# Half-batch loads, pairwise crossbar transposes and a reordered MLP queue in a linear-attention and gated-MLP kernel

## The chip, the cores and the metric

The kernel runs on one core of a Trainium2 chip. A core has a matrix engine (TensorE, PE in the profile, with its weight loads as PEld), a vector engine (VectorE, DVE), an engine for activations (ScalarE, ACT), a general one (GpSimd, POOL) and SyncE (SP), which here only issues DMAs. Each engine runs its own instructions in order and waits on semaphores for the others. The metric is the device time of one execution in microseconds: 302.88 us, the median of three runs (301.88 to 304.17). The profiled execution took 299.19 us and its span, from the first instruction to the last, is 297.4 us.

## What is computed

Attention with a feature map, over 8 batches, 8 heads, 576 tokens and head size 64, and then an MLP whose gate mixes the tokens:

```python
def phi(x):                                    # x: (8, 8, 576, 64), w_phi: (64, 128)
    proj = np.einsum('bhsd,df->bhsf', x, w_phi)
    proj = proj - np.max(np.abs(proj), axis=-1, keepdims=True)
    return np.concatenate([np.exp(proj), np.exp(-proj)], axis=-1)
q_p, k_p = phi(q), phi(k)
kv  = np.einsum('bhsf,bhsd->bhfd', k_p, v)
z   = np.sum(k_p, axis=2)
num = np.einsum('bhsf,bhfd->bhsd', q_p, kv)
den = np.einsum('bhsf,bhf->bhs', q_p, z)[..., None] + 1e-06
x   = (num / den)                              # then heads side by side: (8, 576, 512)

h = np.maximum(x @ w_in, 0.0)                  # w_in: (512, 1024)
u, v = h[..., :512], h[..., 512:]
v_n = (v - mean(v)) / np.sqrt(var(v) + 1e-06)  # over the last axis
v_s = np.einsum('ts,bsd->btd', w_spatial, v_n) + b_spatial[None, :, None]
out = (u * v_s) @ w_out                        # w_out: (512, 512)
```

All inputs and the output are float32 in memory; the kernel computes its matmuls in bfloat16.

## The kernel before

The tokens of a batch are split in a main part of 512 and a tail of 64. Two batches (a group) share one tail tile. The attention is a list of 36 units: a unit is a pair of heads of one batch's main part (four units a batch) or the tail of a group. A software pipeline walks over them in steps, and each step does one stage of several units: the keys and queries of unit i, the sums (kv) of unit i-2, the attention of unit i-3, the output transpose of unit i-4.

```python
units = []
for g in range(G):                       # G = 4 groups of two batches
    if g > 0:
        units.append(dict(pair=False, g=g, i=len(units)))       # tail
    for b in (2 * g, 2 * g + 1):
        for pj in range(NP):             # NP = 4 pairs of heads
            units.append(dict(pair=True, g=g, b=b, pj=pj, i=len(units)))
# ...
ORDER = (("keys", 0.375), ("queries", 0.25), ("attention", 0), ("sums", 0.25),
         ("next", 0.125), ("features", 0), ("out", 0), ("maxima", 0))
LAGS = dict(next=-1, maxima=1, features=2, sums=2, attention=3, out=4)
```

q and k are loaded by GpSimd's DMA queue, which also turns them into bfloat16, one DMA for each operand and batch. v goes through SyncE's queue. From batch 2 on (XB = 2), q and k are transposed by the DMA crossbar, with one transpose for each operand and batch. Batches 0 and 1 and the tails are transposed on TensorE. `pin` is a helper that keeps an instruction in program order, which is why many lines of the profile carry its line, L61.

```python
def pin(start):                                                    # L61
    return lambda *a, **kw: tc.keep_in_program_order(start(*a, **kw))

def alloc(b):
    st[b] = dict(
        q=ld.tile([P, H, NB * D], BF16, tag="q_bf", name="q_bf", bufs=2),
        k=ld.tile([P, H, NB * D], BF16, tag="k_bf", name="k_bf", bufs=2),
        v=ld.tile([P, H * NB, D], FP32, tag="v_f", name="v_f"),
    )

def load(x, b, h0=0, n=H):
    if b not in st:
        alloc(b)
    pin(nc.gpsimd.dma_start)(out=st[b][x][:, h0:h0 + n], in_=main_ap(q if x == "q" else k, b, h0, n))

def cross(b):
    d = st[b]
    for x in ("k", "q"):
        d[x + "T"] = ld.tile([P, 2 * H, P], BF16, tag=x + "T_b", name=x + "T_b", bufs=2)
        pin(nc.sync.dma_start_transpose)(out=d[x + "T"], in_=d[x].rearrange("p h x -> p (h x)"))

def q_even(u):                      # a copy of half of qT, through SyncE's queue
    u["qE"] = qts[u["i"] % len(qts)]
    pin(nc.sync.dma_start)(out=u["qE"][0:D], in_=st[u["b"]]["qT"][0:D, 4 * u["pj"]:4 * u["pj"] + 4, :])
```

The keys and queries are projected on TensorE (`ps`, L247). VectorE takes the maxima of their absolute values (L259, L273), ScalarE the exponentials (`kf` L262, `qf` L346, `em` L282), and GpSimd multiplies v by the key's scale `em` (`vs` L287, the tail's `vst` L302) and prepares the queries' maxima (`mhl` L276, L277). Then come the sums `pv` (L359, L361) and the attention `pn` (L379), the normalization of x on VectorE (L369, L370), and the transpose of x, which for most units is also a crossbar transpose on SyncE's queue:

```python
def a_x_t(u):
    # ...
    dst = st[u["b"]]["xT"][:, u["pj"], :]
    if XX <= u["i"] < NU - 4:                                      # XX = 9, NU = 36
        nc.sync.dma_start_transpose(out=dst.rearrange("p (n t) -> p n t", n=NB),   # L388
                                    in_=u["x"].rearrange("p n h d -> p (n h d)"))
        return
    # ... else four transposes on TensorE and a copy by VectorE (L393, L394)
```

When the last pair of a batch has its x, the batch's MLP goes into a queue of tasks. They are woven between the attention's stages, with the number of tasks for each stage set by their cost. The tasks are v (`pv` L428, relu `vr` L430 on ScalarE, statistics L431 on VectorE), the root and the normalization on GpSimd (`rs` L439, `vn` L445), u (`pu` L482, relu L484 on ScalarE), the spatial matmuls (`ps` L503, L504, times u on VectorE, L506) and the output (`po` L528, copied by L531, stored by L537).

```python
def b_ln(b):
    d = st[b]
    rstd = root(d["mv"], slice(0, P), NB)
    for j in range(NB):
        normalize(d["vn"][:, j, :], d["vr"][j], rstd[:, j, :])     # GpSimd, L445

def b_tasks(b):
    # outs: output tasks of batch b-1; vs, us, ss: four each of v, u, spatial
    ts = outs[:1] + [(MM, lambda: b_v_tail(g, [bl]))] + vs[:2] + outs[1:2] + vs[2:]
    ts.append((0.0, lambda: b_ln(b)))
    ts += outs[2:3] + us[:1] + outs[3:] + us[1:2]
    if b == 0:
        ts += [(0.3, lambda i=i: transpose_spatial(i)) for i in range(NB + 1)]
    ts += us[2:3] + ss[:1] + us[3:] + ss[1:2] + [(MM / 2, lambda: b_u_tail(g, [bl]))] + ss[2:]
    ts.append((MS / 2, lambda: b_s_tail(g, [bl])))
    return ts + (out_tasks(b) if b == B - 1 else [])
```

Loads and crossbar transposes are placed at the ends of steps, counted from the first unit of their batch:

```python
AT, AB, XP = 5, 6, 3
at(1, load, "k", 1)
at(1, load, "q", 1)
at(1, load_v, 1, nc.sync)
# ... weights at steps 2 to 4
for u in units:
    if not u["pair"] and u["g"] > 0:
        at(u["i"] - AT, load_tail, "k", u["g"])
        at(u["i"] - AT + 1, load_tail, "q", u["g"])
        at(u["i"] - AT + 1, load_tail, "v", u["g"])
    if u["pair"] and u["pj"] == 0 and u["b"] > 1:
        at(u["i"] - AB, load, "k", u["b"])
        at(u["i"] - AB + 1, load, "q", u["b"])
        at(u["i"] - AB + 1, load_v, u["b"], nc.sync)
        if u["b"] >= XB:
            at(u["i"] - XP, cross, u["b"])
for u in units:
    if merged(u):
        at(u["i"] - 1, q_even, u)
for i in range(NU + 4):
    step(i)
    for f in io.get(i, []):
        f()
```

Of the kernel before, what the change touches and what calls it, by code (L numbers as in the profile page):

```python
# [8 lines left out]
FP32 = mybir.dt.float32  # L9
BF16 = mybir.dt.bfloat16  # L10
# [6 lines left out]
def kernel(  # L17
# [15 lines left out]
    nc = tc.nc  # L33

    B, H, S, D = q.shape
# [4 lines left out]
    P = 128  # L40
    KC = DM // P
    NP = H // 2
    NB = 4
    T0 = NB * P
    TL = S - T0
# [14 lines left out]
    def pin(start):  # L60
        return lambda *a, **kw: tc.keep_in_program_order(start(*a, **kw))  # L61
# [9 lines left out]
    st = {}  # L71
    gs = {}

    XB = 2

    def alloc(b):
        st[b] = dict(
            q=ld.tile([P, H, NB * D], BF16, tag="q_bf", name="q_bf", bufs=2),
            k=ld.tile([P, H, NB * D], BF16, tag="k_bf", name="k_bf", bufs=2),
            v=ld.tile([P, H * NB, D], FP32, tag="v_f", name="v_f"),  # L80
        )

# [4 lines left out]
            v=ld.tile([P, H, D], FP32, tag="v_tl", name="v_tl", bufs=1),  # L87
        )

    def load(x, b, h0=0, n=H):  # L90
        if b not in st:
            alloc(b)
        pin(nc.gpsimd.dma_start)(out=st[b][x][:, h0:h0 + n], in_=main_ap(q if x == "q" else k, b, h0, n))

    def load_v(b, eng):
        pin(eng.dma_start)(out=st[b]["v"].rearrange("p (h c) d -> p h (c d)", h=H), in_=main_ap(v, b))

    def load_tail(x, g):
        if g not in gs:
# [45 lines left out]
    pin(nc.vector.tensor_scalar)(out=sel, in0=sel1.unsqueeze(2).to_broadcast([P, H, F]), scalar1=-1.0,  # L145
                                 scalar2=None, op0=ALU.mult)
    for x in ("k", "q"):
        pin(nc.vector.tensor_copy)(out=st[0][x][:, 0:2], in_=first[x])
    vst, vnt = [], []
    for i in range(2):  # L150
        t = cpool.tile([P, 2, 2, H, DA], BF16, name=f"vst{i}")
# [10 lines left out]
    load_v(0, nc.sync)  # L162
    for x in ("k", "q", "v"):
        load_tail(x, 0)
    load("k", 0, 2, 2)
    load("q", 0, 2, 2)
    load("k", 0, 4, 4)
    load("q", 0, 4, 4)
# [5 lines left out]
    wspt = ld.tile([TL, S], BF16, tag="kT_b", name="wspt", bufs=2)  # L174
    bsp_row = ld.tile([P, S], FP32, tag="qT_b", name="bsp_row", bufs=2)
# [46 lines left out]

    def q_even(u):
        u["qE"] = qts[u["i"] % len(qts)]
        pin(nc.sync.dma_start)(out=u["qE"][0:D], in_=st[u["b"]]["qT"][0:D, 4 * u["pj"]:4 * u["pj"] + 4, :])

    def a_transpose(u):
        src = st[u["b"]] if u["pair"] else gs[u["g"]]
        if "kT" in src:
            for x in ("kT", "qT"):  # L230
                u[x] = src[x][:, 4 * u["pj"]:4 * u["pj"] + 4, :] if u["pair"] else src[x]
            return
        for x, copy in (("k", nc.vector.tensor_copy if u["i"] < EK else nc.scalar.copy), ("q", nc.vector.tensor_copy)):
            pt = psum.tile([P, 4, P], BF16, tag="bank", name="pt")
            for j in range(4):
                if u["pair"]:
                    blk = src[x][:, 2 * u["pj"] + j // 2, (j % 2) * P:(j % 2 + 1) * P]
# [196 lines left out]
    def root(mv, r, n):  # L434

        var = small.tile([P, NB, 1], FP32, tag="var", name="var")
        rs = small.tile([P, NB, 2], FP32, tag="rs", name="rs")
        nc.gpsimd.tensor_scalar(out=var[r, 0:n], in0=mv[r, 0:n, 1:2], scalar1=1e-6, scalar2=None, op0=ALU.add)
        nc.gpsimd.tensor_tensor(out=rs[r, 0:n, 0:1], in0=var[r, 0:n], in1=neghalf[r, 0:n].unsqueeze(2), op=ALU.pow)  # L439
        nc.gpsimd.tensor_tensor(out=var[r, 0:n], in0=mv[r, 0:n, 0:1], in1=rs[r, 0:n, 0:1], op=ALU.mult)  # L440
        nc.gpsimd.tensor_scalar(out=rs[r, 0:n, 1:2], in0=var[r, 0:n], scalar1=-1.0, scalar2=None, op0=ALU.mult)
        return rs

    def normalize(dst, src, rs):
        nc.gpsimd.tensor_scalar(out=dst, in0=src, scalar1=rs[:, 0:1], scalar2=rs[:, 1:2],  # L445
                                op0=ALU.mult, op1=ALU.add)
# [216 lines left out]
    at(4, load_weight, w_in_bf[:, :, 0:HALF], cols[:, :, 0:HALF])  # L663
    at(4, load_weight, w_out_bf, moe_w_out.rearrange("(kc p) f -> p kc f", p=P))
    for u in units:
        if not u["pair"] and u["g"] > 0:
# [49 lines left out]
```

## Time and profile before

| | |
|---|---|
| median of three runs | 302.88 us (301.88 to 304.17) |
| span of the profiled execution | 297.4 us |
| mean granted TensorE clock | 0.977 |
| GpSimd DMA loads of a whole batch of k or q | 7 + 7, 512 KB each, 8.6 and 8.8 us to landing (median) |
| crossbar transposes of k and q | 6 + 6, 7.1 and 5.6 us to landing (median) |
| crossbar transposes of x | 20, 4.2 us to landing (median) |

"Busy" is the time in which an engine executes; matmuls are pipelined, so a busy PE need not be PE at its peak. The row of the granted clock gives tenths of full speed in 40 slices of the span. A line of a group or a timeline reads: source line, engine, operation, destination <- source, and in brackets the idle time of the engine before it and what ended it. A line of the waits reads: who waited <- for what, the total in us, how many times, and the longest. POOL's or SPq's DMA lines are the issue of a DMA, not the transfer, which is listed as the time to landing.

### The profile page before, as it was taken

The numbers are of one execution on the slowest core, as the hardware profiler recorded it, in microseconds if no ns is written. First come the engines' busy times: TensorE is split into PE (matmuls) and PEld (weight loads), VectorE is DVE, ScalarE is ACT, GpSimd is POOL, SyncE is SP. The second block draws the span as 40 slices with busy tenths as digits, with TensorE's granted clock in tenths as the row PEclk, the third lists the DMA queues.
The fourth block names the chain that finished last, engine by engine and source line by source line (L and its number), as shares of the span: only waits on it lengthen the run. The fifth ranks groups of instructions, "written<-read, shape, count | busy, mean of one in ns | idle before, by whom it ended". The sixth has DMA issues, their size and how long they took to land.

```text
span 297.4 us, 8021 instructions
## 1 busy us (share of the span) xinstructions
PE 259.4 (87%) x3002; PEld 172.6 (58%) x3042; DVE 229.0 (77%) x575; ACT 222.4 (75%) x504; POOL 188.9 (64%) x344
## 2 busy tenths in 40 slices
PE   3277899985999999299999989998999999999893
PEld 2156786761776666066676657565666666554351
DVE  6299998882899989268988978996899987656341
ACT  7669998994499988259888977897789976733421
POOL 8589994399639994736657895589347843421700
PEclk9999999996999999779999999999999999999999
DMA  7979999994824999995906997999422300120205
GB/s 185 234 122 178 210 240 187 137 230 64 127 47 102 227 162 164 175 276 116 210 19 187 219 203 157 250 169 176 101 71 65 99 20 35 73 73 36 106 3 177
DMA packets 83628, 41.90 MB, mean 141 GB/s; under 512 B 50626, under 2 KB 78978, under 8 KB 83588
## 3 DMA queue, kind: packets, MB, share of 16 engines
q1 hardware_dynamic: 56100, 29.90, 45.6%
q0 software_dynamic: 27328, 11.41, 32.4%
q8 instruction: 24, 0.39, 0.6%
q14 instruction: 16, 0.13, 0.1%
q10 hardware_dynamic: 160, 0.07, 0.1%
HBM read 32.85 MB, written 9.44 MB: 142 GB/s over the span
## 4 chain that ended last, share of the span: by engine, by line
PE 52%; POOL 15%; ACT 13%; DVE 8%; DMA 5%; issue 4%; SPq 0%; POOLq 0%; ACTq 0%; DVEq 0%
PE ps L503 9%; PE pv L428 7%; PE po L528 6%; PE pu L482 5%; PE ps L247 5%; ACT kf L262 5%; ACT qf L346 4%; PE pv L359 4%; POOL vn L445 4%; DMA q_tl<-in_q_dram 3%; POOL vst L302 3%; PE pn L379 3%; PE pq L325 2%; PE ps L504 2%; ACT vr L430 2%
## 5 line engine op out<-in xcount | busy, mean ns | idle before, releaser
L287 POOL TENSOR_TENSOR vs<-v_f,em 128x512 bf16<-128x512 f32 x64 | 65.5, 1045 | 28.3 <-ACT em L282 26.9
L262 ACT ACTIVATE kf<-ps 128x512 bf16<-128x512 f32 x144 | 75.8, 637 | 8.1 <-DVE mk L259 7.9
L346 ACT ACTIVATE qf<-pq 128x512 bf16<-128x512 f32 x128 | 66.5, 617 | 7.8 <-PE pq L325 7.3
L259 DVE TENSOR_REDUCE mk<-ps 128x4 f32<-128x512 f32 x72 | 47.8, 678 | 0.9 <-issue 0.2
L273 DVE TENSOR_REDUCE mq<-ps 128x4 f32<-128x512 f32 x62 | 39.8, 680 | 2.0 <-PE ps L247 2.0
L503 PE MATMUL ps<-w_spT,vn 128*128 128x512 bf16 x117 | 34.8, 388 | 7.2 <-POOL vn L445 6.1
L506 DVE TENSOR_TENSOR uT<-ps,uT 128x512 bf16<-128x512 f32 x32 | 22.0, 688 | 22.0 <-PE ps L504 21.8
L428 PE MATMUL pv<-w_in_bf,xT 128*128 128x512 bf16 x116 | 31.3, 384 | 7.0 <-DMA xT<-x 6.1
L430 ACT ACTIVATE vr<-pv 128x512 bf16<-128x512 f32 (+1 forms) x40 | 23.7, 622 | 14.8 <-PE pv L428 12.8
L431 DVE BATCH_NORM_STATS2 stats<-vr 128x6 f32<-128x512 bf16 (+1 forms) x40 | 26.6, 683 | 8.4 <-ACT vr L430 8.0
L482 PE MATMUL pu<-xT,w_in_bf 128*128 128x512 bf16 x120 | 32.3, 382 | 0.5 <-issue 0.2
L528 PE MATMUL po<-w_out_bf,uT 128*128 128x512 bf16 x119 | 31.9, 379 | 0.5
L484 ACT ACTIVATE uT<-pu 128x512 bf16<-128x512 f32 x32 | 19.6, 629 | 15.0 <-PE pu L482 12.9
L359 PE MATMUL pv<-vs,kf 128*128 128x66 bf16 x512 | 24.9, 195 | 0.9 <-ACT kf L262 0.9
L370 DVE TENSOR_TENSOR x<-pn,rc 128x256 bf16<-128x256 f32 x64 | 25.2, 418 | 0.5
L379 PEld LDWEIGHTS <-qf 128*128 128x128 bf16 x512 | 20.7, 98 | 8.2 <-issue 1.4
L445 POOL TENSOR_SCALAR vn<-vr,rs 128x512 bf16<-128x512 bf16 x32 | 24.3, 770 | 0.8
L359 PEld LDWEIGHTS <-kf 128*128 128x128 bf16 x512 | 22.1, 98 | 2.9 <-issue 2.4
L503 PEld LDWEIGHTS <-vn 128*128 128x128 bf16 x128 | 11.7, 98 | 20.3 <-POOL vn L445 11.5
L379 PE MATMUL pn<-kv,qf 128*128 128x66 bf16 x512 | 22.2, 195 | 1.0 <-ACT qf L346 1.0
L428 PEld LDWEIGHTS <-xT 128*128 128x128 bf16 x128 | 12.0, 99 | 18.6 <-DMA xT<-x 6.6
L361 PE MATMUL pv<-vst,kf 128*128 128x66 bf16 x128 | 21.5, 193 | 1.2 <-POOL vst L304 1.2
(128 smaller groups left out, 559.6 us busy)
## 6 DMA issues: line engine op xcount, KB each, us to landing
v_f<-in_v_dram SPq DMA_DIRECT2D x8, 1024.0 KB, 9.9
out_dram<-ob SPq DMA_DIRECT2D x32, 256.0 KB, 2.5
k_bf<-in_k_dram POOLq DMA_DIRECT2D x7, 512.0 KB, 8.6
q_bf<-in_q_dram POOLq DMA_DIRECT2D x7, 512.0 KB, 8.8
qt<-qT_b SPq DMA_DIRECT2D x24, 64.0 KB, 2.8
v_tl<-in_v_dram SPq DMA_DIRECT2D x8, 128.0 KB, 5.9
w_in_bf<-in_moe_w_in_dram POOLq DMA_DIRECT2D x2, 512.0 KB, 8.8
out_dram<-ob SPq DMA_DIRECT2D x8, 128.0 KB, 2.3
```

Of the source, the lines that this page charges most:

```text
L259: nc.vector.tensor_reduce(out=u["mk"][:, hs], in_=pk, axis=AX.X, op=ALU.max, apply_absolute_value=True)
L262: nc.scalar.activation(out=u["kf"][:, s, hs, :], in_=pk, func=AF.Exp, bias=0.0, scale=sc)
L273: nc.vector.tensor_reduce(out=mq[:, 4 * half:4 * half + 4], in_=pq, axis=AX.X, op=ALU.max, apply_absolute_value=True)
L287: nc.gpsimd.tensor_tensor(out=vs[:, s, :, 0:D], in0=st[u["b"]]["v"][:, pj * H:(pj + 1) * H, :], in1=em[:, s, :].unsqueeze(2).to_broadcast( ...
L346: nc.scalar.activation(out=qf[:, s], in_=pq, func=AF.Exp, bias=0.0, scale=sc)
L359: nc.tensor.matmul(out=pv[:, hh, s, :], lhsT=u["kf"][:, s, 4 * hh + c, :], rhs=u["vs"][:, s, 4 * hh + c, :], start=(c == 0), stop=False)
L379: nc.tensor.matmul(out=pn[:, pos, :], lhsT=u["qf"][hh][:, s, pos, :], rhs=d["kv"][:, 2 * u["pj"] + hh, s, :], start=(s == 0), stop=(s == 1))
L428: nc.tensor.matmul(out=pv[r], lhsT=lhs(kc), rhs=w_in_bf[:, kc, HALF:DFF], start=(kc == 0), stop=(kc == KC - 1))
L445: nc.gpsimd.tensor_scalar(out=dst, in0=src, scalar1=rs[:, 0:1], scalar2=rs[:, 1:2], op0=ALU.mult, op1=ALU.add)
L482: nc.tensor.matmul(out=pu, lhsT=w_in_bf[:, kc, dc * P:(dc + 1) * P], rhs=d["xT"][:, kc, :], start=(kc == 0), stop=(kc == KC - 1))
L503: nc.tensor.matmul(out=ps, lhsT=d["vn"][:, sp, cs], rhs=w_spT[:, sp, 0:T0], start=(sp == 0), stop=False)
L528: nc.tensor.matmul(out=po[r], lhsT=lhs(dc), rhs=w_out_bf[:, dc, :], start=(dc == 0), stop=(dc == KC - 1))
```

## The change

It replaces the two rotating whole-batch buffers of q and of k by four half-batch buffers each, taken in turns by name, and loads them by halves, spread over steps. Each pair of heads now has its own crossbar transpose, three steps ahead of its unit, in place of one for the whole batch. v is loaded by halves from batch 2 on. The tails of groups 2 and 3 are loaded one step earlier. In the MLP's queue the normalization is split in four tasks, one ahead of each u task, and all u tasks stand ahead of the spatial ones. The purpose is to free buffers earlier and to shorten what other transfers and GpSimd's other work stand behind.

```diff
     def alloc(b):
         st[b] = dict(
-            q=ld.tile([P, H, NB * D], BF16, tag="q_bf", name="q_bf", bufs=2),
-            k=ld.tile([P, H, NB * D], BF16, tag="k_bf", name="k_bf", bufs=2),
+            q=[None, None], k=[None, None],
 ...
+    def half_tile(x, b, y):
 ...
+        if st[b][x][y] is None:
+            n = f"{x}_bf{(2 * b + y) % 4}"
+            st[b][x][y] = ld.tile([P, 4, NB * D], BF16, tag=n, name=n, bufs=1)
+        return st[b][x][y]
+
+    def load(x, b, y, h0=0, n=4):
+        t = half_tile(x, b, y)
+        pin(nc.gpsimd.dma_start)(out=t[:, h0:h0 + n], in_=main_ap(q if x == "q" else k, b, 4 * y + h0, n))
 ...
-    def cross(b):
-        d = st[b]
-        for x in ("k", "q"):
-            d[x + "T"] = ld.tile([P, 2 * H, P], BF16, tag=x + "T_b", name=x + "T_b", bufs=2)
-            pin(nc.sync.dma_start_transpose)(out=d[x + "T"], in_=d[x].rearrange("p h x -> p (h x)"))
+    def cross(x, u):
+        n = f"{x}T_b{u['b'] % 2}{u['pj']}"
+        u[x + "T"] = ld.tile([P, 4, P], BF16, tag=n, name=n, bufs=1)
+        src = st[u["b"]][x][u["pj"] // 2][:, 2 * (u["pj"] % 2):2 * (u["pj"] % 2) + 2, :]
+        pin(nc.sync.dma_start_transpose)(out=u[x + "T"], in_=src.rearrange("p h x -> p (h x)"))
 ...
-    def b_ln(b):
+    def b_root(b):
+        st[b]["rs"] = root(st[b]["mv"], slice(0, P), NB)
+
+    def b_ln(b, j):
         d = st[b]
-        rstd = root(d["mv"], slice(0, P), NB)
-        for j in range(NB):
-            normalize(d["vn"][:, j, :], d["vr"][j], rstd[:, j, :])
+        normalize(d["vn"][:, j, :], d["vr"][j], d["rs"][:, j, :])
 ...
+        ns = [(0.0, lambda j=j: b_ln(b, j)) for j in range(NB)]
         ts = outs[:1] + [(MM, lambda: b_v_tail(g, [bl]))] + vs[:2] + outs[1:2] + vs[2:]
-        ts.append((0.0, lambda: b_ln(b)))
-        ts += outs[2:3] + us[:1] + outs[3:] + us[1:2]
+        ts.append((0.0, lambda: b_root(b)))
         if b == 0:
             ts += [(0.3, lambda i=i: transpose_spatial(i)) for i in range(NB + 1)]
-        ts += us[2:3] + ss[:1] + us[3:] + ss[1:2] + [(MM / 2, lambda: b_u_tail(g, [bl]))] + ss[2:]
+        for y in range(NB):
+            ts += ns[y:y + 1] + outs[2 + y:3 + y] + us[y:y + 1]
+        ts += [(MM / 2, lambda: b_u_tail(g, [bl]))] + ss
 ...
-    at(1, load, "k", 1)
-    at(1, load, "q", 1)
-    at(1, load_v, 1, nc.sync)
+    at(1, load, "k", 1, 0)
+    at(1, load, "q", 1, 0)
+    at(1, load, "k", 1, 1)
+    at(1, load, "q", 1, 1)
+    at(1, load_v, 1)
 ...
         if not u["pair"] and u["g"] > 0:
-            at(u["i"] - AT, load_tail, "k", u["g"])
-            at(u["i"] - AT + 1, load_tail, "q", u["g"])
-            at(u["i"] - AT + 1, load_tail, "v", u["g"])
-        if u["pair"] and u["pj"] == 0 and u["b"] > 1:
-            at(u["i"] - AB, load, "k", u["b"])
-            at(u["i"] - AB + 1, load, "q", u["b"])
-            at(u["i"] - AB + 1, load_v, u["b"], nc.sync)
-            if u["b"] >= XB:
-                at(u["i"] - XP, cross, u["b"])
+            early = 1 if u["g"] > 1 else 0
+            at(i - AT - early, load_tail, "k", u["g"])
+            for x in ("q", "v"):
+                at(i - AT + 1 - early, load_tail, x, u["g"])
+        if u["pair"] and u["b"] >= XB:
+            if u["pj"] == 0:
+                for n, (x, y) in enumerate((("k", 0), ("q", 0), ("k", 1), ("q", 1))):
+                    at(i - AB + n, load, x, u["b"], y)
+                for y in range(2):
+                    at(i - AB + 1 + 2 * y, load_v, u["b"], y)
+            for x in ("k", "q"):
+                at(i - XP, cross, x, u)
```

(`i` is `u["i"]` in the last part.) Left out: the four half loads of batch 0, the names of two start-up tiles, which move to other buffers (`wspt` to those of `ob`, `bsp_row` to those of `xT`), and the lines in `a_transpose` and `q_even` that read the new tiles.

More of the change, by code (lines that the diff above doesn't have):

```diff
@@ L88, in alloc_tail, with load_v @@
         )
-    def load(x, b, h0=0, n=H):
+    def half_tile(x, b, y):
         if b not in st:
             alloc(b)
-        pin(nc.gpsimd.dma_start)(out=st[b][x][:, h0:h0 + n], in_=main_ap(q if x == "q" else k, b, h0, n))
-    def load_v(b, eng):
-        pin(eng.dma_start)(out=st[b]["v"].rearrange("p (h c) d -> p h (c d)", h=H), in_=main_ap(v, b))
+        if st[b][x][y] is None:
[5 more added lines that the diff above has]
+        pin(nc.gpsimd.dma_start)(out=t[:, h0:h0 + n], in_=main_ap(q if x == "q" else k, b, 4 * y + h0, n))
+    def load_v(b, y=None):
+        if b not in st:
+            alloc(b)
+        h0, n = (0, H) if y is None else (4 * y, 4)
+        pin(nc.sync.dma_start)(
+            out=st[b]["v"][:, h0 * NB:(h0 + n) * NB, :].rearrange("p (h c) d -> p h (c d)", h=n),
+            in_=main_ap(v, b, h0, n))
     def load_tail(x, g):
@@ L147 @@
     for x in ("k", "q"):
-        pin(nc.vector.tensor_copy)(out=st[0][x][:, 0:2], in_=first[x])
+        pin(nc.vector.tensor_copy)(out=half_tile(x, 0, 0)[:, 0:2], in_=first[x])
     vst, vnt = [], []
@@ L161 @@
         vnt.append(t)
-    load_v(0, nc.sync)
+    load_v(0)
     for x in ("k", "q", "v"):
         load_tail(x, 0)
[L165 to L168, printed above, removed]
+    load("k", 0, 0, 2, 2)
+    load("q", 0, 0, 2, 2)
+    load("k", 0, 1)
+    load("q", 0, 1)
     w_in_bf = cpool.tile([P, KC, DFF], BF16)
@@ L173 @@
     wspr = cpool.tile([P, NB, TL], BF16)
-    wspt = ld.tile([TL, S], BF16, tag="kT_b", name="wspt", bufs=2)
-    bsp_row = ld.tile([P, S], FP32, tag="qT_b", name="bsp_row", bufs=2)
+    wspt = s2.tile([TL, S], BF16, tag="ob", name="wspt", bufs=6)
+    bsp_row = s2.tile([P, S], FP32, tag="xT", name="bsp_row", bufs=3)
     nc.sync.dma_start(out=bsp_row[TL:TL + 1, :], in_=moe_b_spatial)
@@ L224, in q_even @@
         u["qE"] = qts[u["i"] % len(qts)]
-        pin(nc.sync.dma_start)(out=u["qE"][0:D], in_=st[u["b"]]["qT"][0:D, 4 * u["pj"]:4 * u["pj"] + 4, :])
+        pin(nc.sync.dma_start)(out=u["qE"][0:D], in_=u["qT"][0:D])
     def a_transpose(u):
+        if u["pair"] and u["b"] >= XB:
+            return
         src = st[u["b"]] if u["pair"] else gs[u["g"]]
[L229 to L232, printed above, removed]
         for x, copy in (("k", nc.vector.tensor_copy if u["i"] < EK else nc.scalar.copy), ("q", nc.vector.tensor_copy)):
@@ L236, in a_transpose @@
                 if u["pair"]:
[L237 removed]
+                    blk = src[x][u["pj"] // 2][:, 2 * (u["pj"] % 2) + j // 2, (j % 2) * P:(j % 2 + 1) * P]
                 else:
@@ L665 @@
     for u in units:
+        i = u["i"]
         if not u["pair"] and u["g"] > 0:
-            at(u["i"] - AT, load_tail, "k", u["g"])
-            at(u["i"] - AT + 1, load_tail, "q", u["g"])
-            at(u["i"] - AT + 1, load_tail, "v", u["g"])
-        if u["pair"] and u["pj"] == 0 and u["b"] > 1:
-            at(u["i"] - AB, load, "k", u["b"])
-            at(u["i"] - AB + 1, load, "q", u["b"])
-            at(u["i"] - AB + 1, load_v, u["b"], nc.sync)
-            if u["b"] >= XB:
-                at(u["i"] - XP, cross, u["b"])
+            early = 1 if u["g"] > 1 else 0
+            at(i - AT - early, load_tail, "k", u["g"])
+            for x in ("q", "v"):
+                at(i - AT + 1 - early, load_tail, x, u["g"])
+        if u["pair"] and u["b"] >= XB:
+            if u["pj"] == 0:
[5 more added lines that the diff above has]
+                at(i - XP, cross, x, u)
     at(7, weights_with_max)
```

## The prediction

> **What bounds the kernel now.** I read the page's engine shares first, then the row of granted TensorE clock, then busy time by stretches, and only then the waits.
>
> ```profile
> span 297.4 us, 8021 instructions
> PE 259.4 (87%) x3002; PEld 172.6 (58%) x3042; DVE 229.0 (77%) x575; ACT 222.4 (75%) x504; POOL 188.9 (64%) x344
> PEclk9999999996999999779999999999999999999999
> ```
>
> PE is busy 259.4 of 297.4 us, so 38 us are idle. Each digit of the clock row is 297.4/40 = 7.4 us. Only two places show a reduced clock: near 67 to 74 us and 119 to 134 us. The busy times of six stretches of 10 us say what stands there (columns: PE, PEld, DVE, ACT, POOL busy, granted clock, DMA share, GB/s):
>
> ```profile
> 60.00:70.00 10.00, 6.67 (x89) 4.90 (x87) 7.06 (x18) 8.89 (x20) 8.91 (x19) 0.93 1.02 211
> 70.00:80.00 10.00, 8.82 (x88) 5.14 (x90) 4.68 (x13) 2.90 (x9) 8.86 (x15) 0.73 0.42 56
> 120.00:130.00 10.00, 3.69 (x42) 2.55 (x41) 3.31 (x10) 2.04 (x6) 6.55 (x11) 0.66 1.30 243
> 170.00:180.00 10.00, 9.01 (x115) 6.06 (x114) 8.16 (x21) 8.06 (x19) 8.56 (x17) 1.00 1.35 211
> 200.00:210.00 10.00, 8.53 (x84) 5.30 (x83) 6.96 (x17) 7.79 (x19) 7.93 (x17) 1.00 1.21 194
> 280.00:290.00 10.00, 8.51 (x68) 4.19 (x69) 3.10 (x5) 2.15 (x4) 2.67 (x4) 1.00 0.08 28
> ```
>
> PE idle is 10 minus the first number: 3.3 + 1.2, 6.3, 1.0, 1.5 and 1.5, together 14.8 us. In the other stretches from 80 to 280 us PE is about 95 to 99% busy: there the kernel is bound by PE and no change of loads helps. The first 30 us (PE 2.9, 5.1 and 7.6 busy) are start-up, with 14.4 us idle. The waits name the holes:
>
> ```profile
> PEld L428 <- DMA xT<-x: 6.6, 1, 6.6
> PE ps L503 <- POOL vn L445: 6.1, 10, 2.3
> POOL k_bf L61 <- DMA kT_b<-k_bf: 7.1, 1, 7.1
> ```
>
> (total us, times, longest). The first is the hole at 120 us, a single wait. The second is ten small waits of the spatial matmuls for normalized v. The third belongs to GpSimd, and the timelines tie it to the second. GpSimd, then SyncE's queue:
>
> ```profile
> 57.00 0.92 POOL L61 DMA_DIRECT2D k_bf<-in_k_dram  x1 [7.09 <-DMA kT_b<-k_bf]
> ...
> 69.87 3.02 POOL L445 TENSOR_SCALAR vn<-vr,rs 128x512 bf16<-128x512 bf16 x4
> ```
>
> ```profile
> 109.84 6.27 SPq L61 DMA_TRANSPOSE kT_b<-k_bf  x1
> 117.17 3.20 SPq L61 DMA_TRANSPOSE qT_b<-q_bf  x1
> 120.42 0.61 SPq L61 DMA_DIRECT2D qt<-qT_b  x1
> 121.13 2.62 SPq L388 DMA_TRANSPOSE xT<-x  x2
> ```
>
> GpSimd stood from 49.9 to 57.0 because the load of batch 3 was put in the buffer that batch 2's crossbar transpose was still reading. It then ran with no pause until 78 us, and the normalizations came out at 69.9 to 72.9, which PE waited for. SyncE is in order: the transpose of batch 2's last x had to stand behind a whole-batch k transpose (issue 6.27 us) and a q transpose (3.20 us) that themselves waited for their loads, so it left at 121.1 and PE stood from 120.5 to 126.6.
>
> **What the Trainium skill says.** "TensorE: Matmul & The Clock Gate", Part 1: after an idle window of about 3.4 us the array drops to half rate and needs about as long of work to return. The trace agrees: after the 6.08 us gap the 16 matmuls of L379 span 1.08 us, against 0.66 us at 112.7 us, and from 127 to 130 the granted clock is 0.51. "DMA: Bandwidth & Descriptors", SWDGE vs HWDGE vs iDMA: a DMA that casts must be issued by GpSimd, whose software builds the descriptors, while transposes go through SP or ACT. So half loads cost GpSimd instructions: in this trace 0.91 us for 8 heads and 0.76 to 0.80 us for 2 or 4 heads at the start, nearly a fixed price. The same page's Rules for kernel authors says to coalesce small transfers, below 64 KB being mostly overhead. The pieces here stay at 128 KB (transposes) and 256 KB (loads). The trace prices a 128 KB transpose by x: about 1.22 us issue and 4.2 us to landing, against about 3.2 us and 4.4 to 7.1 us for 512 KB.
>
> **The change, part by part.**
>
> 1. Four named half buffers per operand. Batch 3 no longer shares with batch 2; in the built program the wait of GpSimd's k load on that crossbar transpose is gone. Removed: 7.1 us of GpSimd wait at 50 us. Those 7.1 us are not on PE's path themselves. What PE pays is 1.7 + 2.3 = 4.0 us around 66 to 71 us (it waited for the maxima mhl, then vn, both on GpSimd) and the low clock after. From 70 to 80 the clock is 0.73, so at most 0.27 x 8.8 = 2.4 us; matmul spacing stretched by waits hides part of it, so I take 1.5. Sum 5.5 us, of which I count 5, as GpSimd also has more to issue.
>
> 2. Transposes by pair. 12 large ones (41.5 us of SyncE issue, added up in its timeline) become 48 of 128 KB: 48 x 1.22 = 58.6 us, 17 us more on a queue with room. In front of the last x of batch 2 there now stand a k piece and a q piece: 2.4 us of issue in place of 9.5. But the q half is loaded one step after k and transposed one step later; a step is 7.2 us (the matmuls of kT of units 10 to 35 begin from 58.9 to 240.1 us, 25 steps) and a q load took 8.8 us to land, so SyncE still waits about 1.6 us per batch at that place. I put the x transpose at 116 to 118 us; with 4.2 us to land it is there at 120 to 122, where PE needs it at 120.5. Of 6.1 us I count 5 as gone, and 1 us of the low clock (2.19 us for the pn and kv matmuls from 126.95, against 1.41 elsewhere, and a few of L428). Sum 6.
>
> 3. Normalization spread, u ahead of spatial, tail loads one step earlier. In the built order the first spatial group moves from ahead of the fourth u to behind u's tail: one group of 0.86 us and the tail's 0.6, so vn may be about 1.5 us later than now before PE feels it. The holes at 170 and 200 (1.0 + 1.5, GpSimd busy 8.6 and 7.9 with loads and vn in the chain) and at 285 (1.5) should shrink: I count 2 of 4.0 us.
>
> 4. Added. k and q loads go from 18 to 32 on GpSimd: 14 x about 0.82 = 11.5 us; busy rises from 189 to about 200. Most falls into idle time (GpSimd is 36% idle), but from 20 to 40 us it is already 99% busy, and two more loads stand there before the weights: I count 1 us. Spatial's four DVE multiplications (0.69 us each) come in one bunch while DVE also serves the attention: 0.5 us. SyncE's new waits: 1 us.
>
> Sum: 5 + 6 + 2 - 2.5 = 10.5 us. From 302.9, the median time, that is 292.4; I say 292.
>
> **Rivals.** *SyncE takes the place of what was removed.* some 157 queue entries in place of 115, two q halves per batch with one step of lead each, and x and output stores behind them. For: the queue already waited 19.7 us for k loads and 11.3 for q loads. Against: each wait is short, outputs have six buffers, x is needed only for a batch's last pair. It would leave the 120 us hole partly open or open it at other batches: 297 to 300. *GpSimd becomes the bound in stages.* For: in 20 to 40 us 9.85 and 9.91 of 10 busy, and 11.5 us more work. Against: it waits 26.9 us for em, which is slack, and spread normalizations keep its bursts short. It would take 3 to 6 us back: 295 to 298. *The holes are closed but PE is not followed.* ACT and DVE are at 8 to 10 of 10 in most full stretches, so v's and u's evacuations come in denser bunches and PE waits in small pieces: 295. *Better than counted.* All 14.8 us and 3 us of clock come back: 285.
>
> **Range and chances.** The likeliest rivals end between 295 and 300, the best case at 285, so 286 to 299 for 8 in 10. Over 2% faster needs less than 296.8, which my sum passes by nearly 5 us; two rivals would miss it. 0.76 faster, 0.18 within 2%, 0.06 slower.
>
> **What would show it.** Right: GpSimd's 7.1 us wait gone; PE idle in the stretches that now stand at 60 to 80 and 120 to 130 below 2 us each; the clock row without a 6 or 7 after start-up; the wait of L428 for xT under 2 us; PE busy total smaller by 2 to 3 us, the matmul count being the same. Wrong: PE waits for xT or kT at several batches (SyncE); vs or mhl from GpSimd ending PE's waits (GpSimd); a PE share below 90% with no single hole (evacuations); or new idle in the first 45 us.

## Result and profile after

The changed kernel takes 284.69 us (median of four runs, 284.03 to 285.03), the kernel before beside it 302.38 us (301.55 to 304.17). The ratio is 0.9405 (95%: 0.9356 to 0.9453). That is 17.7 us less, where 10.5 were predicted, and below the range of 286 to 299.

The head of the page of the changed kernel, and its clock row:

```profile
span 283.1 us, 8126 instructions
PE 256.1 (90%) x3001; PEld 172.2 (61%) x3042; DVE 229.9 (81%) x575; ACT 223.2 (79%) x504; POOL 198.6 (70%) x358
PEclk9999999999999999999999999999999999999999
```

PE is idle 27 us (283.1 - 256.1) in place of 38, and busy for 3.3 us less: no slice has a reduced clock any more. Five stretches that stood in the prediction (columns as there):

```profile
60.00:70.00 10.00, 8.75 (x105) 6.49 (x107) 7.39 (x24) 8.51 (x19) 9.31 (x17) 1.00 1.07 200
70.00:80.00 10.00, 9.89 (x125) 6.90 (x125) 9.33 (x23) 8.81 (x22) 6.30 (x12) 1.00 1.12 123
120.00:130.00 10.00, 9.95 (x99) 6.40 (x98) 9.07 (x23) 9.32 (x22) 9.13 (x18) 1.00 0.95 193
170.00:180.00 10.00, 9.64 (x119) 6.17 (x119) 9.51 (x23) 8.39 (x21) 5.56 (x9) 1.00 1.27 150
200.00:210.00 10.00, 9.90 (x116) 6.62 (x118) 9.02 (x22) 8.03 (x19) 4.51 (x13) 1.00 0.46 98
```

PE's idle time is 1.25, 0.11, 0.05, 0.36 and 0.10 us, together 1.9; before it was 3.3, 1.2, 6.3, 1.0 and 1.5, together 13.3. The waits for xT at 120 us and of GpSimd's load for kT are gone; of the wait for vn this is left (total us, times, longest):

```profile
PEld L513 <- POOL vn L454: 1.2, 2, 0.7
PE ps L513 <- POOL vn L454: 0.4, 1, 0.4
```

L428, L445 and L503 of the kernel before are L437, L454 and L513 here. GpSimd's timeline (start, length) shows the loads set between the normalizations:

```profile
92.31 0.81 POOL L61 DMA_DIRECT2D k_bf<-in_k_dram  x1
...
98.06 0.77 POOL L454 TENSOR_SCALAR vn<-vr,rs 128x512 bf16<-128x512 bf16 x1
98.78 0.87 POOL L61 DMA_DIRECT2D q_bf<-in_q_dram  x1
99.70 1.51 POOL L454 TENSOR_SCALAR vn<-vr,rs 128x512 bf16<-128x512 bf16 x2
```

and SyncE's queue, then PE, where the hole at 120 us was:

```profile
103.28 1.19 SPq L61 DMA_TRANSPOSE kT_b<-k_bf  x1
...
106.68 1.19 SPq L61 DMA_TRANSPOSE qT_b<-q_bf  x1
...
108.61 2.28 SPq L397 DMA_TRANSPOSE xT<-x  x1
```

```profile
118.08 1.89 PE L437 MATMUL pv<-w_in_bf,xT 128*128 128x512 bf16 x7
```

The same three transposes as in the prediction: x leaves at 108.6, not at 121.1, and PE's matmuls of it carry no wait.

### The profile page after: what moved, and what is told of

It is laid out like the page before. It is cut to its first block, busy times and chain, and to the rows that moved or that the text cites. A ratio compares the mean times of both kernels' runs of the same rounds, so it can differ in the third digit from the quotient of the medians.

```text
span 283.1 us, 8126 instructions
## 1 busy us (share of the span) xinstructions
PE 256.1 (90%) x3001; PEld 172.2 (61%) x3042; DVE 229.9 (81%) x575; ACT 223.2 (79%) x504; POOL 198.6 (70%) x358
## 4 chain that ended last, share of the span: by engine, by line
PE 63%; DVE 13%; ACT 11%; DMA 4%; POOL 3%; issue 3%; POOLq 0%; ACTq 0%; DVEq 0%
PE ps L513 9%; PE pv L437 9%; PE po L538 8%; PE pu L492 7%; PE ps L256 7%; PE pv L368 5%; ACT kf L271 5%; DMA q_tl<-in_q_dram 4%; PE pn L388 4%; DVE mk L268 3%; PE pq L334 3%; DVE stats L440 3%; PE ps L514 2%; ACT qf L355 2%; PE pn L416 2%
## 5 line engine op out<-in xcount | busy, mean ns | idle before, releaser
L296 POOL TENSOR_TENSOR vs<-v_f,em 128x512 bf16<-128x512 f32 x64 | 65.5, 1044 | 21.0 <-ACT em L291 19.5
L513 PE MATMUL ps<-w_spT,vn 128*128 128x512 bf16 x116 | 32.4, 379 | 1.1 <-POOL vn L454 0.4
L492 PE MATMUL pu<-xT,w_in_bf 128*128 128x512 bf16 x121 | 31.5, 379 | 0.5 <-issue 0.2
L437 PE MATMUL pv<-w_in_bf,xT 128*128 128x512 bf16 x116 | 30.7, 379 | 0.7
L439 ACT ACTIVATE vr<-pv 128x512 bf16<-128x512 f32 (+1 forms) x40 | 23.5, 615 | 7.3 <-PE pv L437 5.6
L454 POOL TENSOR_SCALAR vn<-vr,rs 128x512 bf16<-128x512 bf16 x32 | 24.3, 768 | 1.1
L541 ACT COPY ob<-po 128x512 f32<-128x512 f32 x18 | 11.0, 613 | 14.8 <-PE po L538 8.6
L311 POOL TENSOR_TENSOR vst<-v_tl,em 64x512 bf16<-64x512 f32 x16 | 16.3, 1038 | 8.6 <-ACT em L291 8.3
```

Source lines behind the costliest of these rows:

```text
L296: nc.gpsimd.tensor_tensor(out=vs[:, s, :, 0:D], in0=st[u["b"]]["v"][:, pj * H:(pj + 1) * H, :], in1=em[:, s, :].unsqueeze(2).to_broadcast( ...
L437: nc.tensor.matmul(out=pv[r], lhsT=lhs(kc), rhs=w_in_bf[:, kc, HALF:DFF], start=(kc == 0), stop=(kc == KC - 1))
L492: nc.tensor.matmul(out=pu, lhsT=w_in_bf[:, kc, dc * P:(dc + 1) * P], rhs=d["xT"][:, kc, :], start=(kc == 0), stop=(kc == KC - 1))
L513: nc.tensor.matmul(out=ps, lhsT=d["vn"][:, sp, cs], rhs=w_spT[:, sp, 0:T0], start=(sp == 0), stop=False)
```

## The experiments

The change was cut into five parts. **N**: the whole-batch tiles of q and k get two named buffers, one for even and one for odd batches, in place of a pool of two. **H**: loads by half batch, k and q into four named buffers (which includes N's effect), v also by halves. **X**: crossbar transposes pair by pair. **M**: the new order of the MLP queue with normalization spread. **T**: tail loads a step earlier. The changed kernel is H+X+M+T. Runs marked with the same letter are of one chip, and their ratios are to the kernel before on that chip (301.04 us on a, 300.81 on b, 302.81 on c, 300.80 on d).

X brings with it the change's move of two start-up tiles to other buffers.

The last four columns were read from the traces, all for the 120 us hole: how long after the issue of k's load GpSimd issues q's (q); how long after it q's load has landed (q in); how long after it SyncE lets the last x of batch 2 go (x); how long PE then stands for xT (wait). Where loads are halves, the first half of k and of q is meant. Median and range are of all runs; the ratio leaves out runs over 1.5% above the fastest of the same kernel (two of four in e2, three in e13).

| run | parts | us (range) | ratio (95%) | q | q in | x | wait |
|---|---|---|---|---|---|---|---|
| before | none | 302.38 (301.55-304.17) | 1 | 10.4 | 21.8 | 25.8 | 6.1 |
| changed | all (H, X, M, T) | 284.69 (284.03-285.03) | 0.941 (0.936-0.945) | 6.5 | 14.4 | 16.3 | 0 |
| e3 (a) | N | 295.85 (291.78-296.39) | 0.977 (0.968-0.985) | 10.4 | 21.5 | 25.4 | 5.6 |
| e4 (a) | N, X | 297.71 (294.32-298.89) | 0.984 (0.976-0.991) | 10.4 | 20.3 | 23.5 | 4.3 |
| e2 (a) | M | 298.86 (294.0-303.15) | 0.977 (0.971-0.984) | 8.1 | 22.4 | 30.1 | 5.4 |
| e1 (a) | H, X, T | 288.59 (288.51-289.38) | 0.957 (0.952-0.962) | 8.7 | 16.8 | 18.7 | 0 |
| e6 (b) | H, X, M | 285.57 (284.34-288.47) | 0.951 (0.944-0.958) | 8.1 | 15.6 | 17.6 | 0 |
| e5 (b) | N, X, M, T | 286.47 (284.88-288.51) | 0.953 (0.947-0.959) | 6.6 | 16.7 | 19.5 | 0 |
| e8 (b) | H, M, T, X by half | 283.16 (282.67-284.74) | 0.943 (0.938-0.947) | 6.5 | 11.9 | 18.0 | 0 |
| e7 (b) | all, GpSimd loaded | 295.81 (295.32-297.31) | 0.985 (0.979-0.991) | 7.2 | 14.3 | 16.2 | 0 |
| e9 (c) | N, X, T | 292.42 (291.1-294.32) | 0.968 (0.960-0.976) | 8.9 | 19.4 | 21.4 | 4.9 |
| e10 (c) | N, M | 289.26 (288.9-292.31) | 0.959 (0.952-0.966) | 8.1 | 22.5 | 30.3 | 5.6 |
| e11 (c) | N, M, T | 283.39 (283.11-283.72) | 0.937 (0.933-0.942) | 6.6 | 15.3 | 19.1 | 0 |
| e12 (c) | all (H, X, M, T) | 283.78 (282.59-285.6) | 0.939 (0.933-0.945) | 6.5 | 13.9 | 15.8 | 0 |
| e13 (d) | N, T | 292.47 (284.83-293.1) | none | 8.9 | 18.0 | 21.7 | 4.7 |
| e14 (d) | M, T | 288.02 (286.41-289.53) | 0.956 (0.948-0.963) | 6.6 | 15.7 | 19.5 | 0 |
| e15 (d) | N, X, M, T | 288.35 (285.06-290.93) | 0.953 (0.944-0.963) | 6.6 | 20.3 | 22.2 | 3.3 |
| e16 (d) | N, M, T | 283.94 (282.56-285.17) | 0.942 (0.935-0.949) | 6.6 | 15.1 | 18.8 | 0 |
| e17 | none | 299.66 (one run) | none | 10.4 | 20.3 | 24.4 | 5.4 |

Two columns carry the finding on this hole: in every trace in which q's load had landed within 16.8 us of k's issue PE did not wait there, and in every one in which it landed after 18.0 us or more PE waited 3.3 to 6.1. In all of them q's transpose was issued within 0.4 us of that landing, and x behind it. When q's load was issued does not tell by itself: e15 waited with 6.6, e1 did not with 8.7.

**e1 and e2: each half of the change alone.** e1 keeps the old `b_ln` and the old order of `ts`; e2 is the kernel before with only these new:

```diff
-        ts.append((0.0, lambda: b_ln(b)))
-        ts += outs[2:3] + us[:1] + outs[3:] + us[1:2]
+        ts.append((0.0, lambda: b_root(b)))
 ...
+        for y in range(NB):
+            ts += ns[y:y + 1] + outs[2 + y:3 + y] + us[y:y + 1]
```

> The changed kernel with the MLP queue of before (one normalization task, spatial woven between u). Theory A (the holes come from the shared buffer and from SyncE standing behind large transposes): nearly all of the gain stays, 285 to 288 us, with at most 2 us more PE wait for vn than in the changed kernel. Theory B (order and spreading of the MLP queue carry half or more): 292 to 296 us, PE waits for vn of 4 us or more, a hole after the third step of batch 0's MLP near 70 us.

> The kernel before with only the new order of the MLP queue: whole-batch loads, shared buffers and whole-batch transposes stay. Theory A: 298 to 301 us; GpSimd's wait of 7 us for the crossbar transpose stays, and so does the wait of 6 us of PE for xT near 120 us. Theory B: 290 to 294 us, PE's waits for vn (6.1 us before) gone and no drop of the clock near 70 us.

The loads' half has most of it (288.59). The order alone gains 2.2 us in the median (298.86), but its four runs are 294.0, 295.45, 302.27 and 303.15, so it is worth between 0.7 and 2.3%; the trace is of the 295.45. In e2 both large waits are still there (k's load for kT 5.7, PE for xT 5.4). In e1 both are gone, and PE waits for vn in nine small pieces, 3.2 us together.

**e3 and e4: named buffers, then pair transposes.**

```diff
-            k=ld.tile([P, H, NB * D], BF16, tag="k_bf", name="k_bf", bufs=2),
+            k=ld.tile([P, H, NB * D], BF16, tag=f"k_bf{b % 2}", name=f"k_bf{b % 2}", bufs=1),
```

(the same for q). e4 adds, from whole-batch tiles:

```diff
-    def cross(b):
+    def cross(x, u):
+        n = f"{x}T_b{u['b'] % 2}{u['pj']}"
+        u[x + "T"] = ld.tile([P, 4, P], BF16, tag=n, name=n, bufs=1)
+        src = st[u["b"]][x][:, 2 * u["pj"]:2 * u["pj"] + 2, :]
+        pin(nc.sync.dma_start_transpose)(out=u[x + "T"], in_=src.rearrange("p h x -> p (h x)"))
```

> The kernel before with the two whole-batch buffers of q and k given to even and odd batches by name, nothing else: GpSimd's load of batch 3 no longer waits for the transpose of batch 2. Theory A, by the first term of the prediction: 5 us less than before, 297 to 298 us, the hole near 66 to 71 us closed and the hole near 120 us unchanged. Theory B: under 2 us gained, since the burst of GpSimd work at 60 to 73 us remains and vn still comes late.

> As e3, with the crossbar transposes by pair of heads, each three steps ahead of its unit, but loads still by whole batch. Theory A: the hole near 120 us closes too, by the second term 6 us less than e3, 290 to 293 us; what is left to the changed kernel is the half loads and the MLP order. If instead the half loads are what frees SyncE, the x transpose near 120 us still waits for a whole k or q load and the time stays within 2 us of e3.

Stretches and waits of e3:

```profile
60.00:70.00 10.00, 10.00 (x126) 7.69 (x123) 9.01 (x26) 9.96 (x23) 9.36 (x17) 1.00 0.76 176
120.00:130.00 10.00, 7.91 (x65) 4.89 (x66) 4.49 (x14) 3.44 (x7) 4.49 (x10) 0.66 1.26 242
```

```profile
PE pv L428 <- DMA xT<-x: 5.6, 1, 5.6
PE ps L503 <- POOL vn L445: 3.5, 10, 0.4
```

The hole at 66 to 71 us is gone with two named buffers for each operand, worth 5.2 us; the one at 120 is untouched. e4 should have closed that one if large transposes made it. Its queue, and PE:

```profile
100.76 1.38 SPq L61 DMA_TRANSPOSE kT_b<-k_bf  x1
109.14 1.19 SPq L61 DMA_TRANSPOSE qT_b<-q_bf  x1
...
112.31 1.24 SPq L386 DMA_TRANSPOSE xT<-x  x1
```

```profile
118.17 0.61 PE L426 MATMUL pv<-w_in_bf,xT 128*128 128x512 bf16 x1 [4.26 <-DMA xT<-x]
```

The two issues ahead of x now cost 1.4 and 1.2 us, yet SyncE stood 6.9 us for q's load, x left 23.5 us after k's issue, and PE waited 4.3. From e3 to e4 x leaves 1.9 us sooner: q's transpose goes when its load is in (21.5 and 20.3 us after k's issue), and of the issue only what stands behind that gets shorter (3.1 to 1.2 us). e4 is not faster than e3. So the size of the transposes was not the main cause.

**e5, e6, e8: the other way round.** e5 is the changed kernel with whole-batch loads, e6 without the early tails (`early = 0`), e8 with transposes by half batch:

```diff
+        if u["pj"] % 2 == 0:
+            d[x + "T", y] = ld.tile([P, 8, P], BF16, tag=n, name=n, bufs=1)
+            pin(nc.sync.dma_start_transpose)(out=d[x + "T", y], in_=d[x][y].rearrange("p h x -> p (h x)"))
```

> The changed kernel with whole-batch loads of q, k and v (two named buffers each), everything else as changed: pair transposes, early tails, new MLP order. If the early tails are what let the x transpose near 110 us leave in time, this is within 1 us of the changed kernel, 285 to 286 us, and the half loads were worth nothing. If the half loads are, SyncE waits 5 us or more for a whole q load there, PE waits 3 to 5 us for xT, and the time is 289 to 292 us.

> The changed kernel with the tails of groups 2 and 3 loaded where they were before. GpSimd's queue then has the two q tail loads (1.5 us) directly ahead of the first q half again. If the tails matter for the hole near 110 us: PE waits 2 us or more for xT and the time is 286.5 to 289 us. If the half loads alone do it: 284.5 to 285.5 us.

> The changed kernel with the crossbar transposes by half batch (256 KB, 24 in place of 48), each where the first pair of its half had it. By the second term of the prediction SyncE's issue ahead of the x transpose grows by about 1.5 to 2.5 us: PE then waits 1 to 3 us for xT near 110 us, 286 to 288 us. If the issue of the transposes never mattered, only the wait for the loads: 284 to 285.5 us.

Each of these parts can be taken out with most of the gain kept: 286.47, 285.57 and 283.16 are 14.3, 15.2 and 17.7 us below the kernel before on that chip, where the changed kernel on two other chips is 17.7 and 19.0 below. e5 shows no wait for xT and a time between the two that were expected. e6 shows no wait at 120 us, but one of 2.3 us for the xT of a later batch, at 178 us. e8, with half as many transposes of twice the size, is as fast as the changed kernel, where 1 to 3 us of waiting were expected from the prediction's second term.

**e7: more work for GpSimd.** After every k and q load of batches 1 to 7, an operation on a spare tile:

```diff
+        if b > 0:
+            pin(nc.gpsimd.tensor_scalar)(out=spare[:, 1, :], in0=spare[:, 0, :], ...)
```

> The changed kernel with one useless GpSimd instruction after each of its 28 half loads from batch 1 on (128x512 bf16, as long as a normalization, 0.77 us): 21.6 us of GpSimd work more, about twice what the change itself added. By the fourth term of the prediction (1 us for 11.5 us) it would cost about 2 us, 286.5 us. If GpSimd's added work lies wholly in its idle time: under 0.7 us. If GpSimd has become a bound: 5 us or more.

28 operations of 0.77 us are 21.6 us, and the time rises to 295.81, 11 us over the changed kernel (284.69, on another chip), where 2 were expected. Its page and waits:

```profile
PE 261.2 (89%) x3042; PEld 173.1 (59%) x3042; DVE 232.4 (79%) x576; ACT 223.5 (76%) x504; POOL 220.5 (75%) x386
```

```profile
PE pt L322 <- POOL mhl L291: 3.9, 2, 2.7
PE ps L518 <- POOL vn L459: 3.6, 7, 1.4
PE pv L373 <- POOL vs L303: 2.5, 2, 1.8
```

GpSimd's results end PE's waits again, 10.0 us together. So GpSimd at 70% is no idle engine: about half of what is put on it here comes out in the time.

**e9 to e12: which part closes the hole at 120 us.** With N as the base, on one chip: X and T, M alone, M and T, and the changed kernel. T is

```diff
+            early = 1 if u["g"] > 1 else 0
+            at(u["i"] - AT - early, load_tail, "k", u["g"])
```

> e4 (named whole-batch buffers, pair transposes, whole loads, old MLP order) with only the early tails added. If the tail loads directly ahead of the whole q load are what kept SyncE and then PE waiting near 115 us (4.3 us in e4): the wait for xT is gone and the time is 290 to 293 us. If the new MLP order closed that hole in e5: the wait stays above 3 us and the time is 296 to 298 us.

> The kernel before with named whole-batch buffers and the new MLP order; whole loads, whole-batch transposes and late tails stay. If the terms of the runs so far simply add (5.2 for the buffers, 2 to 4 for the order): 292 to 294 us with a wait for xT of 4 us or more near 110 to 120 us. If the new order also makes PE ask for xT later, or SyncE's loads earlier: 288 to 290 us and a wait below 2 us.

> e10 with the early tails: neither half loads nor smaller transposes, SyncE still issues a whole k and a whole q transpose (about 9 us) ahead of batch 2's last x. By the second term of the prediction (issue of the large transposes) PE still waits 3 to 6 us for xT: 289 to 292 us. If the lateness of the loads alone made the hole: within 1.5 us of the changed kernel.

> The changed kernel itself on the same chip as the three others, to compare with them: 284 to 285.5 us, PE waits for xT and vn below 1 us.

e11 has neither half loads nor pair transposes and equals the changed kernel: 283.39 beside 283.78. GpSimd and SyncE's queue in e10 (wait 5.6 us):

```profile
90.97 0.93 POOL L61 DMA_DIRECT2D k_bf<-in_k_dram  x1
...
97.61 1.49 POOL L61 DMA_DIRECT2D q_tl<-in_q_dram  x2
99.07 0.93 POOL L61 DMA_DIRECT2D q_bf<-in_q_dram  x1
```

```profile
104.80 8.21 SPq L61 DMA_TRANSPOSE kT_b<-k_bf  x1
113.51 6.27 SPq L61 DMA_TRANSPOSE qT_b<-q_bf  x1
...
121.29 2.56 SPq L388 DMA_TRANSPOSE xT<-x  x2
```

and in e11 (no wait):

```profile
90.94 0.93 POOL L61 DMA_DIRECT2D k_bf<-in_k_dram  x1
...
97.57 1.01 POOL L61 DMA_DIRECT2D q_bf<-in_q_dram  x1
```

```profile
101.47 4.70 SPq L61 DMA_TRANSPOSE kT_b<-k_bf  x1
106.29 3.02 SPq L61 DMA_TRANSPOSE qT_b<-q_bf  x1
...
110.04 3.17 SPq L388 DMA_TRANSPOSE xT<-x  x2
```

The only edit between them is T, which moves the tails of q (1.49 us of issue ahead of q's load in e10), of k and, on SyncE's queue, of v a step earlier. Counted from k's issue, q's load is issued 1.5 us sooner and has landed 7.2 us sooner, since it also takes less time from issue to landing (the last number, in us; e10, then e11):

```profile
q_bf<-in_q_dram POOLq DMA_DIRECT2D x1, 512.0 KB, 14.4
```

```profile
q_bf<-in_q_dram POOLq DMA_DIRECT2D x1, 512.0 KB, 8.7
```

k's load lands sooner too (13.8 us after its issue, then 10.5), so the k transpose is let go 3.3 us sooner; both transposes take less time to issue (7.7 in place of 14.5 us), and x leaves 11.2 us sooner. So most of what T does here is not the 1.5 us of issue. With whole loads and whole transposes k's load took 13.6 to 14.5 us to land in the five traces with late tails (before, e2, e3, e10, e17), and 9.9 to 10.8 in the four with early ones (e11, e13, e14, e16). That late tails are in flight beside these loads is a candidate, not shown; why landings and issues are shorter the profile doesn't say. What M does for the same wait stands in e3 and e10: in e3 four normalizations (3.0 us) and the tail issues (1.5) stand ahead of q's load, in e10 one normalization (0.77) and the same tail issues. The q column falls by 2.3 us with M, by 1.5 with T, by 3.7 with both; but with M alone q's load does not land sooner (q in: 21.5 in e3, 22.5 in e10). M also makes PE ask later: 25.1 us after k's issue in e3, e4, e9 and e13, 27.8 in e2 and e10. Half loads act behind the issue: in e6 q's load is as late as in e10 (8.1), but the transpose of its half leaves 7.6 us after that issue, in e10 that of the whole 14.4. In e9 and e10 the time came as one of the two expectations said and the wait as the other; e10's trace is of the slowest of its four runs (292.31).

**e13 to e16: without M, without N, and two repeats.**

> The kernel before with named whole-batch buffers and early tails, old MLP order. If the new MLP order is needed for the hole near 115 us (the early tails alone did not close it in e9): PE waits 4 us or more for xT, 291 to 296 us. If it was the pair transposes that kept it open in e9: wait below 1.5 us, 286 to 289 us.

> The kernel before with the new MLP order and early tails, but the old shared buffers. If the named buffers matter beyond their own 5 us (GpSimd's wait also makes the later loads late): 294 to 299 us, with GpSimd waiting 5 us or more for a crossbar transpose. If the terms add: 288 to 290 us.

> e5 once more, on the same chip as e16, which differs from it only in transposing whole batches. If pair transposes cost time by themselves, 2 to 3 us more than e16 (286 to 287 us against 283.4); if e5 and e11 differed by their chips, within 1 us of e16.

> e11 once more, on the same chip as e15. If e11's 283.4 us was no accident of its chip, the median is 283 to 284 us again and PE waits below 1 us for xT.

e13's four runs were 292.82, 284.83, 293.1 and 292.13; the trace is of the 292.82 and has a wait of 4.7 us. One kernel gives two times 8 us apart. A race between the load of q and PE would do this, the hole being there in some executions and not in others; the run of 284.83 has no trace, so this is argued. e14 leaves the shared buffers and lacks only N against e16; it is 4.1 us slower, as if the terms added, with the first hole back:

```profile
POOL k_bf L61 <- DMA kT_b<-k_bf: 6.4, 1, 6.4
```

and 2.8 us of waits for vn. e15 and e16 differ only in X: with whole loads it costs 4.4 us in the medians, though one of e15's runs (285.06) lies among those of e16. The profiled execution of e15 took 290.93 us and has a wait of 3.3 us for xT; that of e5, the same kernel, took 284.88 and has none. In e15 the q transpose left 13.7 us after its load was issued, in e5 10.1, in e16 8.5. So in e15 part of the loss is the same hole again; why q is late when transposes are small isn't shown.

**e17: was the profile of before typical?** The kernel before, unchanged.

> The kernel before once more, for a second profile: the one read for the prediction came from an execution of 299.2 us, the fastest of all seen, while the timed ones took 300.2 to 304.2. If the prediction was short because that execution was a lucky one, this profile shows the holes near 66 to 71 and 120 to 126 us longer by 2 us or more in all, or another hole. If the sizes read were typical, the idle time of PE is within 1 us of 38 us.

It took 299.66 us, beside 300.32 for the same kernel; waits for kT of 5.7, for xT of 5.4 and for vn of 6.4 us. The holes are not longer than in the profile read for the prediction but 2 us shorter in all (8.8 us of idle PE from 60 to 80 and 120 to 130 us, 10.8 there), so that execution was no lucky one in its holes. Nor is PE's idle time within 1 us of 38: it is 33.2. Part of this may be that this trace has 3042 matmul records and the other 3002, and a missing record would count as idle.

## Why the prediction missed

The sum of the experiments along one path, in medians, the first two against their own chip's kernel before and the others against their neighbour on one chip: N 5.2 us (301.04 to 295.85); M then 8.3 (e10 gains 13.5, less the 5.2; directly, on two chips, 6.6); T then 5.9 (289.26 to 283.39); half loads and pair transposes -0.4 (283.39 to 283.78). Together 19.0, which is what e12 gains (302.81 to 283.78). The steps depend on their order, as M with T closes the second hole (e11, e14, e16, though in e15, with X, it does not), and H with either does (e1, e6, with X beside it; neither H alone nor H without X was run).

1. *Buffers: 5 predicted.* Right, in mechanism and size: 5.2 us by adding N alone (e3) and 4.1 by lacking N alone (e14 against e16). GpSimd's wait and PE's two waits at 66 to 71 us go, and the clock with them (0.73 to 1.00 from 70 to 80 us). "TensorE: Matmul & The Clock Gate" of the Trainium skill, Part 1, which the prediction used, lets the clock fall after an idle window of about 3.4 us. Here it fell with less (columns as in the other stretches; the clock goes from 1.00 to 0.50):

```profile
65.10:68.50 3.40, 1.62 (x17) 1.08 (x17) 1.72 (x5) 2.77 (x7) 3.09 (x7) 1.00 0.94 165
68.50:71.90 3.40, 1.06 (x2) 0.21 (x2) 1.01 (x2) 2.25 (x6) 3.13 (x6) 0.50 0.29 66
```

In the kernel before PE was still busy for 1.62 us of the 3.4 ahead of the fall at 68.5 us.

2. *Transposes by pair: 6 predicted.* The size of the hole is right, 5.9 us from e10 to e11, but **the step "2.4 us of issue in place of 9.5" failed as a cause**. Pair transposes alone let x go 1.9 us sooner and leave the wait (e4, and with early tails e9: 4.3 and 4.9 us), and whole ones with 7.7 us of issue don't make it (e11). What counts is when q's load is in. The prediction took the median of 8.8 us for its landing; at this place, in the kernel before, it was issued 10.4 us after k's, behind four normalizations and two tail issues, and took 11.4 us to land. SyncE first stood 4.6 us for k's load (14.5 us to landing); k's issue of 6.27 us then ran almost until q's load was in, so that a short issue would only have made SyncE wait for q, as e4 shows. The prediction saw the transposes "that themselves waited for their loads", and took the issue for what mattered. It wasn't the transposes by pair that closed the hole but loads that land sooner, by T with M or by halves; that it closed as counted is luck.

3. *Normalization, order and tails: 2 of 4.0 predicted.* **This is the term that was mis-sized.** The 4.0 us of holes at 170, 200 and 285 us are nine of the ten waits for vn (the tenth, 2.3 us, is in the first hole); from 160 us on the kernel before has

```profile
PE ps L503 <- POOL vn L445: 3.8, 9, 1.1
```

of which 0.4 is left in the changed kernel and in e10: 3.4 gone in place of 2. In the medians M is worth more: 6.6 to 8.3 us on top of N, 8.5 on top of N and T on one chip (e13 to e16), about 4 on top of H, X and T (288.59 in e1 to 284.69, on different chips). With T beside it, M closes the second hole as well (4.7 us of wait in e13, none there in e16). With N alone it doesn't: the traces of e3 and e10 differ in span by 3.7 (294.2 and 290.5), 3.1 of it waits for vn. e10's trace is of its slowest run, so some 3 to 5 us of M's gain on N are not explained by a trace. One candidate is the race: if M lets x arrive in time in some executions, the median falls; it is argued, not shown. T's share, which the prediction put into the same 2 us, is the closing of the hole under 2.

4. *Added costs: -2.5 predicted.* Not there in the sum. e11 makes 14 loads less than e12 and its GpSimd is busy for 9 us less (189.5 us), and the two take the same time (283.39, 283.78). In the first 50 us PE is busy for 33.1 us in the changed kernel and for 34.3 in the kernel before, near the 1 us counted for the start; but without half loads it is anywhere from 32.4 (e15) to 35.2 (e4), so this can't be laid to them. The estimate of GpSimd's busy time, 200, was right (198.6). The prediction also took from "DMA: Bandwidth & Descriptors" of the Trainium skill, Rules for kernel authors, the advice to coalesce small transfers, below 64 KB above all. That size was not tested; pieces of 128 KB cost 4.4 us with whole loads (e15, e16), and nothing that can be measured with half loads (e8).

The two traces that the prediction and the result were read from say by place what was counted and what came:

| place | counted | between the two traces |
|---|---|---|
| PE's waits at 60 to 71 us | 3.5 (4.0, less what was rounded off) | 2.9 (4.0 gone, a new one of 1.1 at 63 us) |
| low clock (PE's busy time) | 2.5 | 3.3 |
| the hole at 120 us | 5 | 6.1 |
| the other waits for vn | 2 | 3.4 |
| costs (PE in the first 50 us) | -2.5 | -1.2 |
| sum | 10.5 | 14.5 (the spans differ by 14.3) |

So about 4 of the 7.2 us by which the prediction fell short lie in these sizes. The rest is that the timed runs of the kernel before are longer than its profiled execution (302.38 and 299.19 us), those of the changed kernel not (284.69 and 284.90): the prediction read its holes in the one and took them from the other.

**The rivals.** SyncE did not become a limit: the changed kernel's trace has no wait of PE for kT or xT after the start. GpSimd did not at this load, and does with 21.6 us more (e7). Denser evacuations: PE's share is 90% without a hole, but its idle time fell with the time. "Better than counted", 285, is what came.

All five signs of being right came: GpSimd's wait, the low clock and the wait for xT gone, PE's idle time below 2 us in each stretch, PE's busy time smaller by 3.3 us (2 to 3 expected). They could not tell the second term's mechanism from another that closes the same hole. Two readings in the prediction were loose: PE is 93% busy from 100 to 110 us, not 95 to 99, and SyncE's waits for loads were not all short (one for k of 13.9 us).

Still open: the 3 to 5 us of M named above; why the timed runs of before are about 3 us longer than its profiled execution; why loads land sooner with early tails; and why q lands later beside small transposes.

## What to carry to other kernels

When an in-order queue stands behind a wait, follow that wait back to what it waits for, to its issue and to its landing at that very place: here the transpose waited for a load that was issued behind 4.5 us of other work on its engine and then took 11.4 us to land, not the median of 8.8. Loading the tails earlier and spreading that work (T and M) gave, with named buffers, all of the gain (e11: 283.39 us), and splitting loads and transposes none on top. Before the issue that fills the time until a landing is shortened, ask what would be waited for next. And read holes and the time from the same executions: here they differed by 3 us.

## What the runs showed of the hardware

- The issue of the same 512 KB crossbar transpose of k took 4.70 us in e11 and 8.21 in e10, while a 128 KB one mostly took 1.2 to 1.5 us. In e10 x stood behind 14.5 us of such issue on SyncE.
- A load that casts costs GpSimd nearly the same for half the bytes: 0.80 us for 256 KB, 0.93 for 512 KB (k's loads at 90 us in e8 and e3). To landing the same 512 KB load of q took 14.4 us in e10 and 8.7 in e11. In the median the halves took 6.7 us (k) and 7.5 (q) in the changed kernel, the whole ones 8.6 and 8.8 in the kernel before.
- The clock can fall without a wholly idle stretch: before the fall at 68.5 us PE was busy for 1.62 of 3.40 us.
- One kernel can have two times: e13 gave 284.83 once and 292.1 to 293.1 three times. A single profile of it tells one of the two.
